# Turning a third diagonal of score blocks by DMA, with z brought in as fp32 and the query copies dropped

## The chip, the cores and the metric

The kernel runs on one core of one Trainium2 chip. The metric is the device time of one execution in microseconds (us). The core's engines are TensorE (PE; its weight loads are shown as PEld), VectorE (DVE), ScalarE (ACT), GpSimd (POOL) and SyncE (SP), which does nothing here but issue DMAs. All DMAs of the core, whichever engine issues them, are carried out by 16 DMA engines.

## The reference

Two layers follow one another, over 8 batches of 3200 tokens, with a width of 256 and a head size of 64:

```python
scores = (1.0 / S) * np.matmul(z, z.transpose(0, 2, 1))        # z: 8 x 3200 x 64
x = u * np.matmul(np.maximum(scores, 0.0) ** 2, v)             # u, v: 8 x 3200 x 256
wq, wk = x @ w_q, x @ w_k                                      # 256 -> 64
mixed = np.einsum('bst,btd->bsd', (1/8) * np.einsum('bsd,btd->bst', wq, wk), x)
out = np.maximum(mixed, 0.0) @ w_out                           # 8 x 3200 x 256, float32
```

The scores of a batch are symmetric, since both factors are z. The second layer has no nonlinearity between its two products, so the kernel sums the keys times x first (a 64 x 256 matrix per batch, called the heads here) and multiplies the queries with that.

## The kernel before

**Tiles.** A batch's 3200 tokens make seven groups of columns, six of 512 and one of 128 (`widths`, numbered 0 to 6; the last is `LASTG`), and 25 rows of 128. A score tile is one row of 128 by one group of columns. For a group, the kernel needs all 25 rows: they are the weights of the second product, in 128x128 pieces, with the matching row of v as the moving operand (L289, 100 matmuls of 256 columns for a group of 512).

**Scored or turned.** Because the scores are symmetric, a block that was scored for group gi and belongs to the rows of group gj serves group gj too, transposed. `is_turned` says for which pairs of groups that is done: up to two groups further on (`FAR`), and for the last group always. Such a block goes through a DMA transpose (L268) from the tile `at` into a tile `tt` (tags tt1 and tt2 by distance, with 3 and 4 buffers; ttl for the last group), and the later group reads its weights from there. All other tiles are scored by PE (L211). The contraction of a score matmul is 64 long, so z is held twice, on both halves of the partitions (`zT`), and the two matmuls of a pair run on the two halves of the array.

**Stages of a pair.** Two score tiles share one PSUM tile (three of them, `pps`). The first stage (DVE L234 or ACT L230) takes the positive part into the fp32 tile `g`; the second stage (POOL L249 or ACT L247), one pass later, squares it into the fp16 tile `at` (14 buffers); then the transposes of its turned blocks are issued on SP.

**The loop.** Nothing is scheduled by the compiler; the program's order is what each engine executes. The main loop makes one pass after another, number k. A pass scores six tiles (four where it also mixes), runs the first stage of these pairs and the second stage of those of the pass before, and lets PE do a share of the second product of the group in hand, on tiles scored two passes before (`LAG`). After ten of its matmuls one further piece of work can stand: a round of keys, or the mixing of one group of the batch before. `at_phase` holds what is due at the start of a pass: loads of u, and loads, doubling and turning of z, and loads of v for the next batch.

**Gate and keys.** When a group is complete, `gate` multiplies the two accumulators with u on DVE (L315), and x is turned by DMA (`xT`, L327). Five passes later or more, `keys_and_heads` projects x to queries and keys (L337), ACT copies them (L348), SP turns the keys (`kx`, L353). In the pass of the next round, `double_keys_queries` copies the queries to the other half of the partitions by a DMA on SP (L361) and the keys within `kx` on POOL (L362); PE then multiplies these keys and x (`heads`, L368), and DVE adds the sums over the groups (L379, L381; after the last group L387 makes `hs`).

**Mixing.** Once a batch's heads are complete, its groups are mixed one by one in the passes of the next batch: two matmuls (L416), one for each half of the width, on the two halves of the array, a ReLU on ACT (L428), the output projection (L441), a scaling (L468 or L463) and the store on SP (L469). The last group of 128 goes beside the key rounds (`side_mix`, `side_proj`).

**z.** The first batch's z is loaded as fp32 in four pieces and turned by PE. Later ones come by one casting DMA on POOL's queue into half of `zd` (L131), DVE doubles it (L134), and SP turns all of it with one DMA transpose (L138). `zd` has one buffer.

**Behind the loop** the last batch's heads come from a Gram matrix of x (`last_gram`, `last_heads`), and the rest of the mixing of the last two batches follows.

## Time and profile before

| | |
|---|---|
| Median of 3 runs | 807.75 us (806.59 to 809.63) |
| The profiled execution | 807.18 us, its span 805.4 us |
| Granted TensorE clock | 0.999 |
| Busy share of PE, DVE, ACT, POOL | 98%, 61%, 59%, 60% |
| Score matmuls (L211) | 920 |
| Second product (L289) | 5000 matmuls of 273 ns: weights from `at` 3656, from `tt` 1152, from `ttl` 192 |
| DMA | 330,878 packets, 143.20 MB; under 512 bytes 307,441 |

The spans are measured from the first to the last instruction. Matmuls overlap in their pipeline, so the mean of one (273 ns) is longer than its distance to the next. "Idle before" is the time in which an engine did nothing ahead of an instruction, with what ended it. The share of the DMA engines adds up the durations of their packets over 16 engines; packets of two queues can overlap, so it can pass 1.

### The profile page before, as it was taken

The page shows a single profiled execution, that of the slowest core. Times are in us where ns is not written, and L with a number is a line of the kernel's source. Part 1 is how long each engine was busy: PE and PEld are TensorE (multiplying, and loading weights), DVE is VectorE, ACT ScalarE, POOL GpSimd, SP SyncE. Part 2 cuts the span into 40 slices and gives each one's busy share as a digit, 9 for nine tenths or more (in the row PEclk, how much of TensorE's full clock was granted, in tenths as well). Part 3 has the DMA queues.
Part 4 walks back from the last instruction along what each step waited for, and adds up shares of the span by engine and source line. Part 5 has one row for each costly group of instructions (what it writes and reads, how often), then busy time and mean ns, then how long its engine had stood idle before and what let it go on. Part 6 is the DMA issues. An engine that isn't in the chain of part 4 may idle for free.

```text
span 805.4 us, 16696 instructions
## 1 busy us (share of the span) xinstructions
PE 788.8 (98%) x6778; PEld 584.9 (73%) x6778; DVE 493.1 (61%) x514; ACT 475.1 (59%) x526; POOL 485.2 (60%) x352
## 2 busy tenths in 40 slices
PE   7999999999999999999999999999999999999996
PEld 4777777777777777777777777777777767767774
DVE  5766666565665566755676556765666656655525
ACT  6655556556765556565675556656665565565534
POOL 7957676564666557755666466864676555655420
PEclk9999999999999999999999999999999999999999
DMA  7999899997989969998899979999999996867436
GB/s 175 149 198 192 141 176 181 212 190 134 216 148 208 200 152 194 176 208 186 175 157 211 198 157 178 188 206 175 184 197 157 182 217 143 159 148 183 116 98 246
DMA packets 330878, 143.20 MB, mean 178 GB/s; under 512 B 307441, under 2 KB 313137, under 8 KB 330801
## 3 DMA queue, kind: packets, MB, share of 16 engines
q1 hardware_dynamic: 302528, 125.90, 76.4%
q0 software_dynamic: 28128, 15.98, 17.7%
q8 instruction: 53, 0.87, 0.5%
q10 hardware_dynamic: 144, 0.26, 0.1%
q14 instruction: 25, 0.20, 0.1%
HBM read 59.38 MB, written 26.21 MB: 106 GB/s over the span
## 4 chain that ended last, share of the span: by engine, by line
PE 95%; issue 1%; POOL 1%; DMA 1%; DVE 1%; ACT 0%; SPq 0%; POOLq 0%; DVEq 0%
PE acc L289 69%; PE sc L211 13%; PE fo L441 5%; PE qk L368 3%; PE qk L337 3%; PE mx L416 2%; POOL at L249 1%; DMA z<-in_z_dram 1%; DMA xT_sb<-x_sb 0%; DVE x_sb L315 0%; DVE fo L463 0%; PE qk L499 0%; ACT qk L348 0%; SPq L95 0%; DVE g L234 0%
## 5 line engine op out<-in xcount | busy, mean ns | idle before, releaser
L249 POOL TENSOR_TENSOR at<-g 128x1024 f16<-128x1024 f32 (+2 forms) x234 | 430.3, 1853 | 222.2 <-DVE g L234 136.8
L234 DVE TENSOR_SCALAR g<-sc 128x1024 f32<-128x1024 f32 (+1 forms) x340 | 388.1, 1184 | 188.5 <-PE sc L211 188.1
L289 PE MATMUL acc<-v_sb,at 128*128 128x256 f16 x3656 | 446.8, 273 | 0.4 <-DVE x_sb L315 0.4
L289 PEld LDWEIGHTS <-at 128*128 128x128 f16 x3656 | 344.7, 98 | 108.0 <-issue 66.6
L230 ACT ACTIVATE g<-sc 128x1024 f32<-128x1024 f32 x128 | 131.2, 1025 | 199.6 <-PE sc L211 199.6
L247 ACT ACTIVATE at<-g 128x1024 f16<-128x1024 f32 (+2 forms) x234 | 236.9, 1029 | 0.6 <-DVE g L234 0.6
L289 PE MATMUL acc<-v_sb,tt 128*128 128x256 f16 x1152 | 149.1, 273 | 0.0
L211 PE MATMUL sc<-zT 64*128 64x512 f16 x920 | 129.7, 381 | 2.3 <-DVE hs L387 0.9
L289 PEld LDWEIGHTS <-tt 128*128 128x128 f16 x1152 | 112.5, 98 | 12.9
L315 DVE TENSOR_TENSOR x_sb<-acc,u_sb 128x512 f16<-128x512 f32 (+1 forms) x104 | 69.3, 668 | 66.8 <-PE acc L289 62.5
L428 ACT ACTIVATE rt<-mx 128x1024 f16<-128x1024 f32 (+1 forms) x49 | 49.1, 1012 | 56.8 <-PE mx L416 55.3
L211 PEld LDWEIGHTS <-zT 64*128 64x128 f16 x920 | 34.9, 95 | 50.1 <-issue 28.5
L362 POOL COPY kx<-kx 128x256 f16<-128x256 f16 (+1 forms) x54 | 20.1, 378 | 65.9 <-DMA kx<-qk 65.7
L468 ACT ACTIVATE fo<-fo 128x1024 f32<-128x1024 f32 (+1 forms) x40 | 40.6, 1014 | 24.4 <-PE fo L441 22.6
L441 PE MATMUL fo<-wo,rt 128*128 128x256 f16 x386 | 49.6, 273 | 1.7 <-DVE fo L463 0.9
L348 ACT CAST qk<-qk 128x512 f16<-128x512 f32 (+1 forms) x54 | 28.7, 545 | 27.5 <-PE qk L368 13.2
L441 PEld LDWEIGHTS <-rt 128*128 128x128 f16 x386 | 37.2, 98 | 7.5 <-ACT rt L428 1.9
L381 DVE TENSOR_TENSOR ha<-ha,qk 128x256 f32<-128x256 f32 x31 | 13.1, 421 | 30.0 <-ACT qk L348 30.0
L368 PE MATMUL qk<-x_sb,kx 128*128 128x256 f16 x191 | 28.4, 273 | 1.9 <-POOL kx L362 1.9
L337 PE MATMUL qk<-xT_sb,wqk 128*128 128x512 f16 (+1 forms) x108 | 29.9, 358 | 0.0
L368 PEld LDWEIGHTS <-kx 128*128 128x128 f16 x195 | 19.0, 98 | 14.2 <-POOL kx L362 2.4
L289 PE MATMUL acc<-v_sb,ttl 128*128 128x256 f16 x192 | 22.6, 273 | 0.0
(47 smaller groups left out, 150.2 us busy)
## 6 DMA issues: line engine op xcount, KB each, us to landing
u_sb<-in_u_dram SPq DMA_DIRECT2D x48, 512.0 KB, 4.8
out_dram<-fo SPq DMA_DIRECT2D x46, 512.0 KB, 4.2
v_sb<-in_v_dram POOLq DMA_DIRECT2D x35, 320.0 KB, 5.7
qk<-qk SPq DMA_DIRECT2D x47, 64.0 KB, 4.0
zd<-in_z_dram POOLq DMA_DIRECT2D x7, 400.0 KB, 8.1
tt<-at SPq DMA_TRANSPOSE x146, 4.3
u_sb<-in_u_dram SPq DMA_DIRECT2D x8, 128.0 KB, 3.0
xT_sb<-x_sb SPq DMA_TRANSPOSE x56, 4.1
```

What stands on the lines that cost most here:

```text
L211: nc.tensor.matmul(out=sc[:, h, 0:gw], lhsT=zT[b][half : half + dqk, ts(ti, P)], rhs=zT[b][half : half + dqk, ds(gs, gw)], start=True, sto ...
L230: nc.scalar.activation(out=g[:, hs, 0:w], in_=sc[:, hs, 0:w], func=RELU, scale=GSCALE)
L234: nc.vector.tensor_scalar(out=g[:, hs, 0:w], in0=sc[:, hs, 0:w], scalar1=0.0, scalar2=GSCALE, op0=AOP.max, op1=AOP.mult,)
L247: nc.scalar.square(out=out, in_=g[:, hs, 0:w])
L249: nc.gpsimd.tensor_mul(out=out, in0=g[:, hs, 0:w], in1=g[:, hs, 0:w])
L289: nc.tensor.matmul(out=accs[j // 2][:, ds((j % 2) * D, D)], lhsT=weights(b, gi, ti, j), rhs=vs[b][:, ti, :], start=(first and ti == rows_[ ...
L315: nc.vector.tensor_mul(out=xs[b, gi][:, 2 * half : 2 * half + n, :].rearrange("p n d -> p (n d)"), in0=accs[half][:, 0 : n * D], in1=us[b, ...
L337: nc.tensor.matmul(out=out, lhsT=w[:, ac, :, :].rearrange("p t h -> p (t h)"), rhs=xTs[b, gi][:, 0 : gw // P, ac, :], start=(start and ac ...
L368: nc.tensor.matmul(out=ps[:, 1, 0:D], lhsT=ks[b, gi][:, n, :, :].rearrange("p a h -> p (a h)"), rhs=xs[b, gi][:, n, :], start=((gi, n) == ...
L428: nc.scalar.activation(out=rts[b, gi][:, :, 0:gw], in_=ps[:, :, 0:gw], func=RELU)
L441: nc.tensor.matmul(out=banks[jf // 2][:, ds((j - jf) * D, D)], lhsT=rt[:, dc, ts(j, P)], rhs=wo[:, dc, :], start=(dc == 0 and j == jf), st ...
L468: nc.scalar.mul(out=flat_out[:, sl], in_=part, mul=FINAL_SCALE)
```

## The change

- Blocks three groups further on are turned too, except in the last batch. All three distances now have `tt` tiles of three buffers. In a group's order of tiles, the blocks for the next group stand first, then those that only this group uses and those for groups further on; the last row fills the pair up.
- z of batches 1 to 7 comes as fp32 on SP's queue, in four pieces of six or seven rows; DVE casts each piece twice, into the two halves of a smaller `zd` of one buffer, after the first stages of a pass (`late`); SP turns each piece a pass later. The first batch's z is doubled in tiles of `at`'s pool.
- In odd groups and the last one the projection's weights are swapped (`wkq`), so the queries land on the other half of the partitions. The copies of queries and keys (`double_keys_queries`) are gone; the heads of even and odd groups are summed on different halves and added crosswise at the end of the batch (`heads_crossed`), with `hz`, half of it zero, for the last group.
- Mixing takes two groups side by side, one half of the width at a time; the two matmuls use the two halves of the array for the two groups. A mixing pass projects one finished group of `todo_proj`.
- The loads of v stand two passes earlier. The pools of `g` and `rt` have fewer buffers, the raw weights lie in a tile of x's pool, and the part behind the loop follows the new mixing.

The core of the diff:

```diff
@@ pools and the first batch's z @@
-    FAR = 2
-    pg = ctx.enter_context(tc.tile_pool(name="pg", bufs=8))
+    pg = ctx.enter_context(tc.tile_pool(name="pg", bufs=7))
-    prt = ctx.enter_context(tc.tile_pool(name="prt", bufs=3))
+    prt = ctx.enter_context(tc.tile_pool(name="prt", bufs=2))
+    ZP = [(0, 6), (6, 6), (12, 6), (18, 7)]
-    zd0 = pz.tile([P, NT, 2, dqk], FP16, tag="zd", name="zd")
...
+        zds[c] = pat.tile([P, nn, 2, dqk], FP16, tag="at", name="zd")
...
@@ z of the later batches @@
-    def load_z(b):
-        zds[b] = pz.tile([P, NT, 2, dqk], FP16, tag="zd", name="zd")
-        nc.gpsimd.dma_start(out=zds[b][:, :, 0, :], in_=rows(z, b))
-
-    def double_z(b):
-        nc.vector.tensor_copy(out=zds[b][:, :, 1, :], in_=zds[b][:, :, 0, :])
-
-    def turn_z(b):
-        zT[b] = pzt.tile([P, S], FP16, tag="zT2", name="zT2")
+    def load_z(b, i):
+        n0, nn = ZP[i]
+        z32[b, i] = pz.tile([P, 7, dqk], FP32, tag="z32", name="z32", bufs=2)
+        nc.sync.dma_start(out=z32[b, i][:, 0:nn, :], in_=rows(z, b)[:, n0 : n0 + nn, :])
+
+    def double_z(b, i):
+        nn = ZP[i][1]
+        zds[b] = pz.tile([P, 7, 2, dqk], FP16, tag="zd", name="zd")
+        for half in range(2):
+            nc.vector.tensor_copy(out=zds[b][:, 0:nn, half, :], in_=z32[b, i][:, 0:nn, :])
+
+    def turn_z(b, i):
+        n0, nn = ZP[i]
+        if i == 0:
+            zT[b] = pzt.tile([P, S], FP16, tag="zT2", name="zT2")
         nc.sync.dma_start_transpose(
-            out=zT[b][:].rearrange("p (n s) -> p n s", s=P),
-            in_=zds.pop(b)[:].rearrange("p n a k -> p (n a k)"),
+            out=zT[b][:, ds(n0 * P, nn * P)].rearrange("p (n s) -> p n s", s=P),
+            in_=zds[b][:, 0:nn, :, :].rearrange("p n a k -> p (n a k)"),
         )
...
@@ which blocks are turned, and the order of a group's tiles @@
-    def is_turned(gi, gj):
-        return gi < gj and (gj <= gi + FAR or gj == LASTG)
+    def is_turned(b, gi, gj):
+        far = 3 if b + 1 < B else 2
+        return gi < gj and (gj <= gi + far or gj == LASTG)
...
-            elif len(tiles) % 2:
-                order = own[:1] + near + own[1:]
             else:
-                order = near + own
+
+                single = [NT - 1]
+                order = [t for t in near if group_of(t) == gi + 1 < LASTG]
+                order += [t for t in own + near if t not in order + single]
+                order = single + order if len(tiles) % 2 else order + single
...
-                kind, nr, bufs = ("l", 1, 8) if gj == LASTG else (gj - gi, 4, gj - gi + 2)
+                kind, nr, bufs = ("l", 1, 8) if gj == LASTG else (gj - gi, 4, 3)
...
@@ keys, queries, heads @@
-        ks[b, gi] = pk.tile([P, 4, 2, dh], FP16, tag="kx", name="kx")
+        ks[b, gi] = pk.tile([P, 4, P], FP16, tag="kx", name="kx")
...
-    def double_keys_queries(b, gi):
-        gw = widths[gi]
-        nn = gw // P
-        nc.sync.dma_start(out=qks[b, gi][dh:P, 0:gw], in_=qks[b, gi][0:dh, 0:gw])
-        nc.gpsimd.tensor_copy(out=ks[b, gi][:, 0:nn, 0, :], in_=ks[b, gi][:, 0:nn, 1, :])
+    def swapped(gi):
+        return gi % 2 == 1 or gi == LASTG
...
     def heads_out(b, gis, ps):
+        mine = slice(0, dh) if swapped(gis[0]) else slice(dh, P)
...
+        acc, part = hacc[b][mine, :], ps[mine, 1, 0:D]
+        if gis[0] < 2:
+            nc.vector.tensor_copy(out=acc, in_=part)
         else:
-            heads_done(b, ps[:, 1, 0:D])
...
+            nc.vector.tensor_add(out=acc, in0=acc, in1=part)
+
+    def heads_crossed(b):
+
+        hx = psml.tile([P, D], FP32, tag="hx", name="hx", bufs=1)
+        nc.vector.tensor_copy(out=hx[0:dh, :], in_=hacc[b][dh:P, :])
+        nc.vector.tensor_copy(out=hx[dh:P, :], in_=hacc[b][0:dh, :])
+        return hx
+
+    def heads_done(b):
+        hx = heads_crossed(b)
         hss[b] = psml.tile([P, D], FP16, tag="hs", name="hs")
-        nc.vector.tensor_add(out=hss[b][:], in0=hacc.pop(b)[:], in1=part)
+        nc.vector.tensor_add(out=hss[b][:], in0=hacc.pop(b)[:], in1=hx[:])
+        nc.vector.tensor_copy(out=hz[b % 2][dh:P, :], in_=hss[b][dh:P, :])
...
@@ mixing @@
-    def mix(b, gi):
-        gw = widths[gi]
+    def mix(b, pair, db):
+
+        ps = ps_tile("mx")
+        for a in range(2):
+            half = a * dh
+            nc.tensor.matmul(
+                out=ps[:, a, :],
+                lhsT=hss[b][half : half + dh, ds(db * P, P)],
+                rhs=qks[b, 2 * pair + a][half : half + dh, :],
+                start=True,
+                stop=True,
+            )
+        return ps
...
@@ group_begun: what a batch's first pass makes due @@
-            due(k + later + 3, lambda: load_z(b + 1))
-            due(k + later + 9, lambda: double_z(b + 1))
-            due(k + later + 10, lambda: turn_z(b + 1))
+            for i, at in enumerate((1, 3, 6, 8)):
+                at += k + later // 4
+                due(at, lambda i=i: load_z(b + 1, i))
+                due(at + 3, lambda i=i: double_z(b + 1, i), late)
+                due(at + 4, lambda i=i: turn_z(b + 1, i))
             for i in range(5):
-                due(k + later + 5 + 3 * i, lambda i=i: load_v(b + 1, 5 * i, 5))
+                due(k + later + 3 + 3 * i, lambda i=i: load_v(b + 1, 5 * i, 5))
...
@@ the loop @@
-        if keying and keyed:
-            for g_ in keyed[0][1]:
-                double_keys_queries(keyed[0][0], g_)
         if mixing:
             mix_out(*mixing)
+            if mixing[2] == 1:
+                todo_proj.extend((mixing[0], 2 * mixing[1] + a) for a in range(2))
         staged = []
         act_pair = 0 if (gate_pending or k < 4) else 1
         for i, (p0, sc) in enumerate(fresh):
             on_act = i == act_pair and not mixing
             staged.append((p0, first_stage(p0, sc, on_act)))
+        for fn in late.pop(k, []):
+            fn()
...
-        if mixing:
-            mb, mg, _ = mixing
+        if mixing and todo_proj:
+            mb, mg = todo_proj.pop(0)
...
@@ behind the loop @@
+    for _ in range(min(2, len(todo_mix))):
+        mix_next()
+    psh = ps_tile("hd")
+    last_heads(last, g32, psh)
+    hss[last] = psml.tile([P, D], FP16, tag="hs", name="hs")
+    nc.vector.tensor_add(out=hss[last][:], in0=hx[:], in1=psh[:, 1, 0:D])
+    while todo_mix:
+        mix_next()
...
+    for pair in range(LASTG // 2):
+        for db in range(ND):
+            mix_out(last, pair, db, mix(last, pair, db), on_dve=(pair == 0 and db == 1))
+            if pair:
+                store(last, 2 * pair - 2 + db)
```

## The prediction

> **What bounds the kernel now.** First the page's engine line and the chain that ended last: is one engine busy throughout, and doing what?
>
> ```profile
> PE 788.8 (98%) x6778; PEld 584.9 (73%) x6778; DVE 493.1 (61%) x514; ACT 475.1 (59%) x526; POOL 485.2 (60%) x352
> PE 95%; issue 1%; POOL 1%; DMA 1%; DVE 1%; ACT 0%; SPq 0%; POOLq 0%; DVEq 0%
> PE acc L289 69%; PE sc L211 13%; PE fo L441 5%; PE qk L368 3%; PE qk L337 3%; PE mx L416 2%; POOL at L249 1%; DMA z<-in_z_dram 1%; DMA xT_sb<-x_sb 0%; DVE x_sb L315 0%; DVE fo L463 0%; PE qk L499 0%; ACT qk L348 0%; SPq L95 0%; DVE g L234 0%
> ```
>
> TensorE is the bound; DVE, ACT and POOL have 40% to spare. So a score matmul saved is time saved, if what replaces it (a DMA transpose) arrives in time. Next, therefore, the DMA side: the slices, the queues, one stage of the windows, and the issues.
>
> ```profile
> DMA  7999899997989969998899979999999996867436
> q1 hardware_dynamic: 302528, 125.90, 76.4%
> q0 software_dynamic: 28128, 15.98, 17.7%
> 220.00:320.00 100.00, 100.00 (x867) 74.31 (x865) 61.53 (x65) 60.44 (x67) 62.02 (x44) 1.00 1.01 181
> tt<-at SPq DMA_TRANSPOSE x146, 4.3
> zT<-zd SPq DMA_TRANSPOSE x7, 6.8
> qk<-qk SPq DMA_DIRECT2D x47, 64.0 KB, 4.0
> zd<-in_z_dram POOLq DMA_DIRECT2D x7, 400.0 KB, 8.1
> ```
>
> Behind a PE that never waits, the 16 DMA engines are full as well (share 1.01 in a steady stage). Last, SP's queue in the order of time, in the third batch (start, us, instruction), and one round of keys from the timeline of all engines:
>
> ```profile
> 221.40 2.49 SPq L353 DMA_TRANSPOSE kx<-qk  x2
> 223.94 0.57 SPq L146 DMA_DIRECT2D u_sb<-in_u_dram  x1
> 224.61 9.53 SPq L268 DMA_TRANSPOSE tt<-at  x4
> 234.23 1.23 SPq L268 DMA_TRANSPOSE ttl<-at  x1
> ...
> 246.09 3.99 SPq L138 DMA_TRANSPOSE zT<-zd  x1
> ...
> 255.48 0.59 PE L337 MATMUL qk<-xT_sb,wqk 128*128 128x512 f16 x2
> ...
> 265.69 1.22 SPq L353 DMA_TRANSPOSE kx<-qk  x1
> ...
> 268.19 0.40 POOL L362 COPY kx<-kx 128x256 f16<-128x256 f16 x1 [5.31 <-DMA kx<-qk]
> ...
> 271.26 0.60 PE L368 MATMUL qk<-x_sb,kx 128*128 128x256 f16 x4
> ```
>
> SP issues without a pause here. The turn of zT belongs to the pass of the main loop whose first score starts at 239.3; SP gets to it at 246.09, 6.8 us late, and three passes on it is 9.8 us late (a copy due at 253.6 is issued at 263.44). The keys projected at 255.5 reach SP at 265.7, land near 268.2, and are multiplied at 271.3: 3 us to spare. PE is not waiting, but SP's queue is close to being what it waits for.
>
> **The gain.** Tiles scored per batch by group are now 25, 21, 17, 17, 17, 17, 1 = 115. Turning also three groups further takes four each from groups 3, 4 and 5: 103. It holds for batches 0 to 6: 7 × 12 = 84 of 920 score matmuls go. Six of them take 0.75 us from their start to the next product (268.98 to 269.73 in PE's timeline), so 84 × 0.125 = 10.5 us; at the chain's 13.5% of 805.4 / 920 = 118 ns it would be 9.9. The second product keeps its count, only its operand comes from `tt` instead of `at` (both rows 273 ns). Mixing has as many matmuls as before. DVE, ACT and POOL lose 42 pairs, off the path.
>
> **Edits on other engines.** POOL loses 54 copies of kx (20 us) and seven z issues (1.6 us each). DVE gets 56 small casts of z (an fp32 128x256 cast took 294 ns; near 0.4 us each, 22 us) for seven copies of 1.34 us, which hide in its 39% idle time unless they wait (below). Crossing the two halves of the heads adds two copies and an add ahead of the first mix, at 0.42 us each 1.26 us; in the trace hs ends 1.26 us ahead of that matmul in five of seven batches, so 0 to 0.3 us each: nothing taken, 2 us in the range. The tail has one more group of the batch before to project and store (0.87 us on PE, which leaves the loop); its pairs need both ReLUs before the first store: +0.5 us net, 0 to 2. The smaller pools (7 `g`, two pairs of `rt`) only matter when a reader is late; taken at nothing.
>
> **The DMA balance.** By the trace's packet records a 256-byte packet takes 24.8 ns on average. A 128x1024 transpose is 1024 of them over 16 engines: 1.58 us; the 42 new ones are 66 us of all 16 engines. z leaves POOL's queue (22,400 packets of 128 bytes, 35.5 ns: 50 us) and comes as fp32 on SP's (3,584 packets at the 90 ns of the first batch's z: 20 us); the 54 copies of q (61 ns a packet) take 11.5 with them. Net +25 us over seven batches, but SP's own queue, served in order, gets +75.
>
> The Trainium skill, "DMA: Bandwidth & Descriptors", section Specifications, gives about 27 GiB/s per engine and warns that transfers under 512 bytes stay below line rate. At its full rate the new transposes would cost an estimated 24 us, not 66. The rows side with the warning: 256 bytes in 24.8 ns are 10 GB/s, 4096-byte loads run at 20 (200 ns).
>
> **Where it bunches.** The new blocks are made by groups 0 to 2 of each batch, in which group 0 and 1 passes are the shortest on PE. I count the fourth batch from the second pass of group 0 to the second of group 2, nine passes. PE: 240 second-product matmuls at 112.5 ns (32 take 3.60 in the chain) 27.0, scores 9 × 0.75 = 6.8, two mixes and three key rounds 4.5: 38.3 us. SP's queue: 18 tt 28.4, two ttl and four kx at 0.79 4.7, two xT 3.2, two of z's turns 2.5, four z loads 2.8, three u 4.8, two stores 3.2: 49.6, and three v loads beside them on POOL's queue, 7.1: 56.7 us of packets. How fast does that go? From 209.8 to 246.1 packets worth 40.4 us went out in 36.3, a ratio of 0.90; from 240.15 to 278.6, 40.7 in 38.5, 0.95. So 51 us, 13 more than PE has, where the same group of passes before ended 7 us late. Lower bound: if only issue counts (tt 1.29, kx 1.22, loads 0.4 to 0.6 us), 43 us, 5 more.
>
> **What waits for that.** Two things. First the keys: the kx of the sixth of these passes has 35.8 us of packets ahead of it, 32.2 us at 0.90, against 20.4 us of PE; with 1 us of lateness at the start it is issued 12.8 us after its pass begins, lands (median 3.4) at 16 to 17, and the heads want it at 15: PE waits about 2 us, more directly than before, as POOL's copy no longer stands between. Second a new wait: z's pieces share one `zd` buffer, so DVE's cast of a piece waits until the turn of the piece before has landed, and on DVE the gates, the head sums and the next pass's first stages queue behind it. The last cast stands one pass after the third turn. Late by 12 us (13 and 1, less the 2 already waited) and landing 3.5 after issue, that turn is done 15.5 us after its pass starts; DVE comes to the cast at 8.7 (5.7 of the pass, 3.0 to the end of the first stages in the next): 6.8 us late. Of that some 2.5 are DVE's idle gap in a pass (2.0 to 2.7 in the timeline); about 4 reach PE through the score buffers. By 0.90 a batch loses 6 us; by 0.95 8; by issue alone 0, the lateness then fitting the gap. I take 5, nearer the rows of a full queue. In groups 3 to 5 SP has 28 us of work in 36 and recovers.
>
> **Sum.** The profiled execution was 807.18 (span 805.4). 807.18 − 10.5 + 7 × 5 + 0.5 = 832.2. The median of the runs is 0.57 above the profiled one: 832.8, say 833. 0.5%, 4 us, is about what a measurement of this kernel can tell from no change.
>
> **Rivals.**
> *The queue copes.* The stall is nil, as with issue alone; for it: PE waits for no DMA today with SP up to 10 us late, new blocks are needed groups later, and copies of q and the slow 128-byte packets are gone. Against: the counted bunch and the single `zd`. It decides while SP is under 7.7 us late at the third turn (8.7 + 2.5 − 3.5). 807.75 − 10.5 + 0.5 = 797.8, down to 796 with nothing lost in the tail. Chance 0.26. By the skill's 27 GiB/s this is how it would come out; 10 GB/s in the rows bears that out little.
> *It cancels.* 1 to 2 us a batch: 804 to 812. Chance 0.06.
> *DMA sets the pace altogether.* At 0.95 and with `at` buffers held by late transposes (POOL and ACT then wait too), 8 us a batch: 854, with the heads' 2 us 856. Chance 0.18 inside the slower case; it decides where a transpose lands over about 19 us after its second stage, when the fourteenth next pair, 4.7 passes of 4.1 us on, needs the buffer.
> *It doesn't do what it says:* the `tt` two groups on have three buffers, not four; if the fourth block waits for the first's reading, SP's whole queue stands behind it. By the order of tiles the reading is a pass earlier, so this adds to the slower case and has no number of its own.
>
> **How the numbers follow.** Slower 0.68 (0.50 the forecast, 815 to 848; 0.18 the last), same 0.06, faster 0.26. Range 796 to 857: the low end takes in the coping queue, the high end the DMA-bound case.
>
> **What would show it.** Right: L211 x836; its saved time matched by new PE idle time in groups 1 to 3 of each batch, ended by DMA kx or by DVE's g; DVE waiting at the cast of zd on a DMA zT, some 7 us at the last piece; SP late by over 10 us there. Wrong: PE at 98% or more and a span near 796, or DVE's cast never waiting. If PE waits for hs or in the tail instead, the mechanism is another.

## The result, and the profile after

The changed kernel takes 880.73 us (median of six runs, 871.94 to 886.13), the kernel before 809.31 in the same comparison: a ratio of 1.0855, interval 1.0808 to 1.0902. The forecast was 833, its range ended at 857. The direction was right, the size was not: a loss of 71 us where 25 were expected. The profiled execution took 872.33 us, near the lower end of the six; its span is 870.5. Here and in the tables below, a run more than 1.5% above its kernel's fastest counts in the median and not in the ratio.

The page of the changed kernel, the same parts as before (engines; granted clock and DMA by slices; the two queues; the chain that ended last):

```profile
PE 795.3 (91%) x6694; PEld 590.3 (68%) x6694; DVE 497.4 (57%) x566; ACT 438.1 (50%) x493; POOL 420.2 (48%) x273
...
PEclk9998999999999999999999999998999989999999
DMA  8999778985999759998599996999769996688536
...
q1 hardware_dynamic: 347264, 139.45, 76.9%
q0 software_dynamic: 5616, 13.11, 11.0%
...
PE 65%; DVE 6%; DMA 6%; issue 4%; ACT 2%; SPq 1%; DVEq 0%; ACTq 0%
PE acc L305 47%; PE sc L227 8%; PE fo L496 4%; DMA zT<-zd 4%; DVE g L250 2%; PE qk L390 2%; PE qk L356 2%; PE mx L448 1%; DMA kx<-qk 1%; DVE zd L138 1%; DVE x_sb L331 1%; SPq L284 1%; DVE fo L518 1%; ACT at L263 1%; DMA kx<-ql 0%
```

PE is no longer busy throughout, and the chain now runs through the turn of z (4%) and the transposed keys. The 16 DMA engines are not fuller than before: the slices dip to 5 and 6 once a batch. Something waits in a circle, and then nobody has work.

The groups (in each line, behind the second bar, the idle time of the engine before the group and what ended most of it):

```profile
L227 PE MATMUL sc<-zT 64*128 64x512 f16 (+1 forms) x836 | 120.7, 384 | 20.4 <-DVE g L250 9.9
L138 DVE CAST zd<-z 128x384 f16<-128x384 f32 (+1 forms) x56 | 33.8, 645 | 93.3 <-DMA zT<-zd 70.8
L390 PE MATMUL qk<-x_sb,kx 128*128 128x256 f16 x191 | 30.5, 286 | 13.6 <-DMA kx<-qk 12.2
L356 PE MATMUL qk<-xT_sb,wkq 128*128 128x512 f16 x46 | 15.3, 419 | 20.0 <-DVE g L250 20.0
```

The 84 score matmuls are gone (836). DVE stands idle for 93.3 us ahead of the casts of z: 13 us a batch. PE, in turn, waits for DVE's first stages (scores and projections take their PSUM tiles from the same pool, and a tile is free again when its first stage is done) and for the keys. The waits (in total, times, longest, all in us but the count):

```profile
DVE zd L138 <- DMA zT<-zd: 70.8, 13, 11.1
...
DVE zd L138 <- issue: 22.5, 5, 10.2
...
PE qk L356 <- DVE g L250: 20.0, 3, 7.2
PEld L390 <- DMA kx<-qk: 14.5, 5, 5.5
...
PE qk L390 <- DMA kx<-qk: 12.2, 4, 5.0
PE sc L227 <- DVE g L250: 9.9, 5, 5.9
```

SP's queue in the fourth batch, where it issues from 327 to 404 us with no pause of more than some tenths (start, us, instruction):

```profile
347.62 1.88 SPq L144 DMA_TRANSPOSE zT<-zd  x1
349.56 0.63 SPq L152 DMA_DIRECT2D u_sb<-in_u_dram  x1
350.28 7.15 SPq L284 DMA_TRANSPOSE tt<-at  x3
...
366.46 1.24 SPq L144 DMA_TRANSPOSE zT<-zd  x1
...
376.38 7.27 SPq L284 DMA_TRANSPOSE tt<-at  x3
383.75 2.12 SPq L375 DMA_TRANSPOSE kx<-qk  x1
385.96 1.24 SPq L144 DMA_TRANSPOSE zT<-zd  x1
...
395.14 1.25 SPq L144 DMA_TRANSPOSE zT<-zd  x1
```

And one of its gaps, from the timeline of all engines:

```profile
384.62 0.60 PE L305 MATMUL acc<-v_sb,tt 128*128 128x256 f16 x4
...
385.96 1.24 SPq L144 DMA_TRANSPOSE zT<-zd  x1
...
388.82 1.15 DVE L138 CAST zd<-z 128x448 f16<-128x448 f32 x2 [8.64 <-DMA zT<-zd]
...
389.88 2.35 DVE L250 TENSOR_SCALAR g<-sc 128x1024 f32<-128x1024 f32 x2
...
391.14 1.01 PE L356 MATMUL qk<-xT_sb,wkq 128*128 128x512 f16 x2 [5.93 <-DVE g L250]
```

This is the circle. The third turn is issued at 385.96 and lands 2.8 us later; DVE had been waiting 8.64 us for it, with the first stages of the pass queued behind the cast; PE waits 5.9 us for those. The first three turns are issued 19 us apart, though the pieces are planned two or three passes (8 to 14 us) apart. The first turn took 7.3 us to land, at 354.9, and the second cast starts at 355.0; the second landed at 369.2, and the third cast starts at 369.3. So in this batch every piece but the first waits for the turn ahead of it, and each of the next two turns stands behind eight or nine other transposes in SP's queue. Over all seven batches the last piece always waits, 7.2 to 11.1 us and 65 of the 93 us together; the two pieces ahead of it wait in eleven of fourteen cases, 28 us together. The waits that the list puts down to "issue" end with the landing of a turn too.

One more loss is in the clock: 0.974 of the full clock in the profiled execution, where before it was 0.999. Around the gap just shown (a stretch, its length, busy us of PE, PEld, DVE, ACT and POOL with counts, then granted clock, DMA share, GB/s):

```profile
384.00:391.00 7.00, 1.22 (x12) 0.94 (x11) 2.18 (x3) 1.88 (x2) 0.00 (x0) 0.84 0.96 182
391.00:394.00 3.00, 2.85 (x13) 1.81 (x13) 1.34 (x3) 0.59 (x1) 2.77 (x2) 0.50 1.05 203
394.00:397.00 3.00, 3.00 (x22) 2.38 (x21) 1.00 (x2) 1.33 (x2) 0.97 (x1) 0.73 0.59 117
```

PE idles for 6 us and then works at half the clock for some microseconds. The trace has eight such spells ahead of the end, some 41 us together; before had none there. So the engine lines give the whole account. PE's work at nearly the full clock is 779.4 us (its busy time in e15 below, with as many matmuls at a clock of 0.995; e7 has 779.8), 9.4 less than the 788.8 of before: the gain, forecast as 10.5. The changed kernel has 795.3: 15.9 more, most of it by the slow clock: in all its slow spells, with the one at the very end, PE is busy for 27 us, and half of that is 13.5. Its idle time is 870.5 − 795.3 = 75.2 us against 16.6: 58.6 more. −9.4 + 15.9 + 58.6 = 65.1, the difference of the two spans.

### The profile page after: what moved, and what is told of

The parts are those of the page before. It is cut to its first block, busy times and chain, and to the rows that moved or that the text cites. A ratio compares the mean times of both kernels' runs of the same rounds, so it can differ in the third digit from the quotient of the medians.

```text
span 870.5 us, 16494 instructions
## 1 busy us (share of the span) xinstructions
PE 795.3 (91%) x6694; PEld 590.3 (68%) x6694; DVE 497.4 (57%) x566; ACT 438.1 (50%) x493; POOL 420.2 (48%) x273
## 4 chain that ended last, share of the span: by engine, by line
PE 65%; DVE 6%; DMA 6%; issue 4%; ACT 2%; SPq 1%; DVEq 0%; ACTq 0%
PE acc L305 47%; PE sc L227 8%; PE fo L496 4%; DMA zT<-zd 4%; DVE g L250 2%; PE qk L390 2%; PE qk L356 2%; PE mx L448 1%; DMA kx<-qk 1%; DVE zd L138 1%; DVE x_sb L331 1%; SPq L284 1%; DVE fo L518 1%; ACT at L263 1%; DMA kx<-ql 0%
## 5 line engine op out<-in xcount | busy, mean ns | idle before, releaser
L265 POOL TENSOR_TENSOR at<-g 128x1024 f16<-128x1024 f32 (+1 forms) x212 | 392.4, 1862 | 411.2 <-DVE g L250 253.2
L250 DVE TENSOR_SCALAR g<-sc 128x1024 f32<-128x1024 f32 (+2 forms) x309 | 356.2, 1195 | 136.8 <-PE sc L227 135.6
L305 PE MATMUL acc<-v_sb,at 128*128 128x256 f16 x3320 | 412.1, 275 | 6.9 <-DVE x_sb L331 6.8
L305 PEld LDWEIGHTS <-at 128*128 128x128 f16 x3320 | 315.2, 98 | 107.2 <-issue 70.1
L246 ACT ACTIVATE g<-sc 128x1024 f32<-128x1024 f32 (+2 forms) x117 | 116.2, 995 | 237.1 <-PE sc L227 235.1
L305 PE MATMUL acc<-v_sb,tt 128*128 128x256 f16 x1488 | 189.8, 276 | 0.0
L305 PEld LDWEIGHTS <-tt 128*128 128x128 f16 x1488 | 147.8, 99 | 18.7
L227 PE MATMUL sc<-zT 64*128 64x512 f16 (+1 forms) x836 | 120.7, 384 | 20.4 <-DVE g L250 9.9
L138 DVE CAST zd<-z 128x384 f16<-128x384 f32 (+1 forms) x56 | 33.8, 645 | 93.3 <-DMA zT<-zd 70.8
L469 ACT ACTIVATE rt<-mx 128x1024 f16<-128x1024 f32 x47 | 48.0, 1023 | 65.2 <-PE mx L448 64.8
L390 PE MATMUL qk<-x_sb,kx 128*128 128x256 f16 x191 | 30.5, 286 | 13.6 <-DMA kx<-qk 12.2
```

The source lines that it names most:

```text
L138: nc.vector.tensor_copy(out=zds[b][:, 0:nn, half, :], in_=z32[b, i][:, 0:nn, :])
L227: nc.tensor.matmul(out=sc[:, h, 0:gw], lhsT=zT[b][half : half + dqk, ts(ti, P)], rhs=zT[b][half : half + dqk, ds(gs, gw)], start=True, sto ...
L246: nc.scalar.activation(out=g[:, hs, 0:w], in_=sc[:, hs, 0:w], func=RELU, scale=GSCALE)
L250: nc.vector.tensor_scalar(out=g[:, hs, 0:w], in0=sc[:, hs, 0:w], scalar1=0.0, scalar2=GSCALE, op0=AOP.max, op1=AOP.mult,)
L265: nc.gpsimd.tensor_mul(out=out, in0=g[:, hs, 0:w], in1=g[:, hs, 0:w])
L305: nc.tensor.matmul(out=accs[j // 2][:, ds((j % 2) * D, D)], lhsT=weights(b, gi, ti, j), rhs=vs[b][:, ti, :], start=(first and ti == rows_[ ...
```

## The experiments

Each is timed against the kernel before on the same chip; the ratio has its 95% interval in brackets. "Before" and "after" name the kernel that was edited.

**1. Four kernels: the single buffer, the third diagonal, z's way, and the third diagonal alone.**

e1: after, z's doubled pieces in `at`'s pool (14 buffers) in place of the single `zd`.

```diff
-        zds[b] = pz.tile([P, 7, 2, dqk], FP16, tag="zd", name="zd")
+        zds[b] = pat.tile([P, 7, 2, dqk], FP16, tag="at", name="zd")
```

> The changed kernel, but each piece of z is cast into a tile of the pool of `at` (14 buffers) in place of the single `zd`. Theory A (the single buffer is the cost): DVE's 93 us of waits at the cast vanish, the clock returns to 0.99 or more, and the time is 797 to 805 us. Theory B (SP's queue and the DMA engines have more work from group 0 to 2 than PE): the waits at the cast vanish too, but PE then waits for keys (kx), for late blocks or for `at` buffers, SP's queue still runs without a pause for some 70 us of each batch, and the time is 830 to 870.

e2: after, without the third diagonal.

```diff
-        far = 3 if b + 1 < B else 2
+        far = 2
```

> The changed kernel with blocks up to two groups further turned, as before (42 transposes fewer, 84 score matmuls more); z, q, mixing and pools stay changed. Theory A: the cast still waits for each turn of z, so most of the loss stays: over 840 us. Theory B: with the transposes gone SP keeps up, each turn lands before the next cast, and the time is 805 to 815.

e3: after, z as before: one casting load by POOL, one doubling copy on DVE, one turn.

```diff
-            for i, at in enumerate((1, 3, 6, 8)):
...
+            due(k + later + 3, lambda: load_z(b + 1))
+            due(k + later + 8, lambda: double_z(b + 1), late)
+            due(k + later + 9, lambda: turn_z(b + 1))
```

> The changed kernel with z of later batches as before: one casting DMA on POOL's queue, one doubling on DVE, one turn on SP; the third diagonal stays. No piece waits for another. Theory A: 797 to 805 us. Theory B: SP has four loads less but the 128-byte packets are back on the same DMA engines: 830 to 870 us, with PE waiting for keys.

e4: before, with the third diagonal and nothing else of the change but the three buffers for each `tt` tag (the tag two groups on had four).

```diff
-    def is_turned(gi, gj):
-        return gi < gj and (gj <= gi + FAR or gj == LASTG)
+    def is_turned(b, gi, gj):
+        far = 3 if b + 1 < B else 2
+        return gi < gj and (gj <= gi + far or gj == LASTG)
```

> The kernel before with the third diagonal alone (batches 0 to 6; three buffers for each distance), its order of tiles and all else as before. Theory A: 797 to 802 us, as nothing waits for zd. Theory B: SP's queue, with the copies of q still in it, falls further behind than in the changed kernel: 840 us or more, POOL's copies of kx and PE waiting for DMA.

| | us | ratio |
|---|---|---|
| e1 | 850.09 | 1.0533 [1.0481, 1.0585] |
| e2 | 842.81 | 1.0437 [1.0394, 1.0480] |
| e3 | 865.90 | 1.0624 [1.0557, 1.0692] |
| e4 | 835.67 | 1.0346 [1.0291, 1.0401] |

e1: the casts no longer wait for a turn, and the kernel gains some 30 us. So taking the single buffer away is worth 30 us, and e1 is still 41 over the kernel before. What waits now (e1, the waits):

```profile
PEld L390 <- DMA kx<-qk: 29.8, 11, 4.8
...
PE qk L390 <- DMA kx<-qk: 24.4, 11, 4.3
```

The keys, eleven times instead of four: with one circle opened, SP's queue and the DMA engines are what is late.

e4 tells why. It has no new wait at DVE, and still the third diagonal alone costs 27 us. Its DMA engines by slices, its stage from 420 us on, and its waits:

```profile
DMA  8999799999999989999999999999999999877536
```

```profile
420.00:520.00 100.00, 97.81 (x836) 73.49 (x835) 56.27 (x59) 54.91 (x62) 53.78 (x40) 0.98 1.14 197
```

```profile
POOL kx L363 <- DMA kx<-qk: 180.2, 35, 12.4
...
PE qk L369 <- POOL kx L363: 19.4, 7, 6.5
PE sc L212 <- DMA zT<-zd: 7.0, 1, 7.0
```

The slices have no gap left between the batches; the share is 1.14 in this stretch, the highest of seven such stretches (0.98 to 1.14, where before had 0.88 to 1.08); both queues of e4 together hold 82.4 + 18.0 = 100.4% of the 16 engines over the whole span (before 94.1%). In us that is 832 against 758: 74 more, and the prediction had 66 for the new transposes. Before had 47 us left in its span. The prediction's rival of the `tt` buffers has hardly a sign here: of SP's waits ahead of the blocks' transposes one, of 3.1 us, ends with PE's reading.

e3 shows that z's new way is not the root: with z back on POOL's queue and only one turn a batch, PE waits 45.1 us for keys. (Its profiled execution took 870.06 us, of runs from 853.80 to 870.70, so these waits are read for their kind.)

e2 came out where theory A had it, over 840: without the third diagonal the kernel is still 34 us slower than before. DVE's waits at the cast are down from 93.3 to 27.9 us, in nine waits, and each of them ends some 0.1 us after the landing of a turn, those too that the list puts down to "issue". The same line shows a second suspect, the casts themselves:

```profile
L138 DVE CAST zd<-z 128x384 f16<-128x384 f32 (+1 forms) x56 | 44.8, 841 | 27.9 <-issue 20.7
```

0.84 us each where 0.4 were forecast, 45 us of DVE in the middle of its passes.

**2. The casts off DVE, and packets taken away.**

e5: e2, with z as in e3.

> The changed kernel without the third diagonal and with z as before (POOL's casting DMA): what is left are the swapped queries and keys, the crossed heads, mixing by pairs, the smaller pools, v two passes earlier. Theory B (the transposes and z's pieces cost, the rest doesn't): 803 to 812 us. Theory C (the crossed heads and the pairs cost as well, since e2 was still 35 us above the kernel before): 820 us or more.

e6: e2, with e1's buffers and the casts on ACT.

```diff
-            nc.vector.tensor_copy(out=zds[b][:, 0:nn, half, :], in_=z32[b, i][:, 0:nn, :])
+            nc.scalar.copy(out=zds[b][:, 0:nn, half, :], in_=z32[b, i][:, 0:nn, :])
```

> As e2 (two groups further, z in four pieces on SP's queue), but each piece is cast by ACT in place of DVE, into tiles of the pool of `at`. If e2's loss is DVE's (casts of up to 2 us and waits for the turn ahead of gates and first stages): 803 to 815 us. If it is the four loads and turns in SP's queue: 825 to 845.

e7: e1, with v loaded for the first batch alone.

```diff
+        vs[b] = vs[0]
+        return
```

> As e1, but v is loaded for the first batch alone and used for all (POOL's 35 loads of v are left out, so the sums of later batches are not the reference's). If the 16 DMA engines are the limit in groups 0 to 2: packets fall by 7 us in 57 per window, SP's issues return to 1.29 us, waits for kx shrink to a third or less, 805 to 820 us. If SP's issuing alone is the limit: the time stays within 1.5% of e1's 850.

e8: e1, with the casts on ACT and the pieces of z later in the batch.

```diff
-            for i, at in enumerate((1, 3, 6, 8)):
+            for i, at in enumerate((5, 6, 9, 10)):
```

> The third diagonal with z's pieces in tiles of `at`'s pool, cast by ACT, and loaded, cast and turned four to five passes later (loads due at 5, 6, 9, 10), towards groups 3 to 5 where SP has room. By theory B the window of groups 0 to 2 loses some 5 us of z's DMAs: 815 to 835 us, waits for kx about half of e1's. If the time stays at 845 or more, z's place in the queue does not matter.

| | us | ratio |
|---|---|---|
| e5 | 825.26 | 1.0180 [1.0126, 1.0234] |
| e6 | 819.58 | 1.0144 [1.0115, 1.0172] |
| e7 | 810.93 | 1.0036 [1.0019, 1.0053] |
| e8 | 859.85 | 1.0634 [1.0608, 1.0660] |

e5 is at 820 or more, as theory C had it: what is left of the change costs something too. e6, between its two forecasts, is 23 us faster than e2 with the same DMAs in the same places: that much of e2's loss was DVE casting, and waiting to cast. As e6 takes the single buffer away with the casts, it does not part the two. On ACT a cast takes 0.52 us with little spread, and no wait of PE in the loop passes 2.5 us:

```profile
L138 ACT CAST zd<-z 128x384 f16<-128x384 f32 (+1 forms) x56 | 26.4, 521 | 0.5 <-DMA z<-in_z_dram 0.5
```

e7 is the clearest. SP issues the same 522 DMAs as in e1, the matmuls are the same, DVE casts as slowly (843 ns); only 35 loads are missing, and those are on POOL's queue. 39 us come back. The same hundred microseconds as above, in e1 and then in e7:

```profile
420.00:520.00 100.00, 96.94 (x830) 72.86 (x829) 61.20 (x69) 53.44 (x60) 49.74 (x32) 0.98 1.02 200
```

```profile
420.00:520.00 100.00, 99.89 (x869) 75.55 (x867) 66.01 (x72) 56.88 (x64) 50.32 (x29) 1.00 0.94 189
```

The time that SP spends issuing falls from 667 to 622 us, with the same instructions: a transpose took 1.69 us to issue in e1 on average, 1.54 in e7 (the median is near 1.28 in both). So SP is slowed by packets of another queue, and not by the number of its own instructions.

That does not make the 16 engines full throughout. The two queues of e1, and then those of e17 (section 5, a kernel with one new block and z as before):

```profile
q1 hardware_dynamic: 347264, 139.45, 82.3%
q0 software_dynamic: 5616, 13.11, 10.9%
```

```profile
q1 hardware_dynamic: 317312, 129.57, 80.1%
q0 software_dynamic: 28128, 15.98, 18.2%
```

e1's make 93.2% of its span of 845.9, or 788 us, which would fit into the 805.4 of before; e17's make 98.3% of 808.7, or 795 us, and e17 loses nothing. So the sum over the span accounts for e4, and not for e1. Why e1 loses 41 us at a load that e17 carries, no run here separates: the place of the new blocks, z's way and the rest of the change all differ. (e7 also leaves out the issuing of the 35 loads on POOL, 0.6 us each, 21 us of an engine that idles half the time.)

e8 came out above its first forecast: placed later, the pieces come too late, and PE waits for them (15.6 us, four times) beside the keys (20.1 us). Nothing was won.

**3. The parts one by one, and the mended kernel.**

e9: before, with z as fp32 on SP in four pieces, cast by ACT into tiles of `at`'s pool.

> The kernel before with one part of the change: z of later batches as fp32 by SP's queue in four pieces, but cast by ACT into tiles of `at`'s pool. It takes 50 us of 128-byte packets off the DMA engines and adds 20 us on SP's queue. If the DMA engines' load is what matters: no stall, 802 to 809 us, DMA share of a steady stage 0.95 or less. If SP's queue order matters more: keys land later than before, 812 to 825.

e10: e9, with two of the three new blocks (1 to 4, 2 to 5).

```diff
+        third = b + 1 < B and gj == gi + 3 and gi != 0
+        return gi < gj and (gj <= gi + FAR or gj == LASTG or third)
```

> As e9, and two of the three blocks a third group on are turned too (groups 1 to 4 and 2 to 5; 28 transposes or 44 us of DMA more, 56 score matmuls or 7 us of PE less). Load on the engines 14 us over the kernel before: if a full DMA side is the limit, 805 to 820 us, the gain of 7 eaten; if the freed packets carry it, 797 to 803, faster than both.

e11: e1, with the casts on ACT and v's loads later.

```diff
-                due(k + later + 3 + 3 * i, lambda i=i: load_v(b + 1, 5 * i, 5))
+                due(k + later // 2 + 5 + 3 * i, lambda i=i: load_v(b + 1, 5 * i, 5))
```

> The whole change mended where the runs showed waits: z's pieces in tiles of `at`'s pool and cast by ACT (as e8, but loaded at the change's own passes 1, 3, 6, 8), and v loaded about two passes later, as before. The third diagonal stays. If the DMA engines are the limit in groups 0 to 2: 825 to 845 us, waits for kx still over 15 us, as only their order changes. If the waits were DVE's: 800 to 812.

e12: e5, with v's loads where they were before.

```diff
-                due(k + later + 3 + 3 * i, lambda i=i: load_v(b + 1, 5 * i, 5))
+                due(k + later + 5 + 3 * i, lambda i=i: load_v(b + 1, 5 * i, 5))
```

> As e5 (swapped queries, crossed heads and pairs alone), with v loaded at the passes of before. If e5's waits for kx come from v's loads standing earlier: 810 to 818 us, kx waits under 3 us. If not: within 0.5% of e5's 825.

| | us | ratio |
|---|---|---|
| e9 | 812.22 | 1.0103 [1.0061, 1.0146] |
| e10 | 835.41 | 1.0353 [1.0332, 1.0373] |
| e11 | 848.55 | 1.0523 [1.0499, 1.0548] |
| e12 | 814.99 | 1.0102 [1.0080, 1.0123] |

Before was 806.38 in this comparison. z's new way alone costs 5.8 us even with the casts off DVE (e9), just inside what its expectation had if SP's queue order matters more than the load: its two queues hold 746 us of packets, before 758. e12, which keeps of the change the queries' halves, the crossed heads, the pairs of groups, the order of the tiles and the smaller pools, with z's copy and turn planned one pass earlier, costs 8.6. What PE waits for most there, after the start of the program:

```profile
PE mx L442 <- DVE hs L412: 3.9, 3, 1.4
```

That is the crossing ahead of the first mix: up to 1.4 us each time, 3.9 of the 8.6, where the prediction took nothing and kept 2 us in its range; the rest is not traced to one part. Against e5 it also says that v two passes earlier costs 6 us by the ratios, 10 by the medians.

Four terms then add up: the third diagonal 27.1 (e4), z 5.8 (e9), the rest 8.6 (e12), the single buffer 880.73 − 850.09 = 30.6; together 72.1, measured 71.4. Two kernels test the sum in part: without the third diagonal and the single buffer it gives 820.8, and e6 has 819.6; with all but the single buffer 847.9, and e11 has 848.6. It is a ledger of costs found by separate edits, and that it closes so well is partly chance. The terms are not independent: z's new way costs 5.8 us without the third diagonal, and with it e14 (below) is 22 us faster than e13, which has z as before. The ledger also has no entry for v two passes earlier (6 us against e5) and none for the casts on DVE, which cannot be told from the single buffer in e2, and of which nothing can be seen between e1 and e11, which moves v as well.

e10 and e11 missed both their forecasts, upwards. e10: two thirds of the blocks, with z's new way, cost as much as e4 with all of them, although its profiled execution has the two queues at 91.7% of the span. e11: with the waits at the casts taken away and v later, PE waits for keys 34.0 us. Mending these waits did not bring the time back.

**4. Is it the keys, or the packets?** The keys are the one DMA that PE wants within two passes of its issue. If only they were late, it would do to want them later.

e13: e4, with the heads using the keys of two rounds back, and buffers to match.

```diff
-    px = ctx.enter_context(tc.tile_pool(name="px", bufs=5))
-    pk = ctx.enter_context(tc.tile_pool(name="pk", bufs=3))
+    px = ctx.enter_context(tc.tile_pool(name="px", bufs=6))
+    pk = ctx.enter_context(tc.tile_pool(name="pk", bufs=4))
...
-        if keyed:
+        if len(keyed) > 1:
```

> As e4 (the kernel before with the third diagonal alone), but the heads take the keys of two rounds ago, not of one (six passes or more after the projection in place of three; one more buffer each for x, kx and the queries, one fewer for g). If PE's waits for kx (19 us of e4's 32 us of gaps, with the clock they lower) are where the third diagonal's gain goes: 797 to 812 us. If the DMA side is simply too slow, the wait moves to zT, x's turn or the blocks, and the time stays at 825 or more.

e14: e13, with z as in e9.

> As e13, with z in four pieces on SP's queue, cast by ACT into tiles of `at`'s pool (as e9): some 30 us of packets less. If packets decide: 3 to 10 us faster than e13. If SP's order decides: as e13 or slower.

e15: e4, with v loaded for the first batch alone, as in e7.

> As e4, with v loaded for the first batch alone and used for all batches (35 loads of v left out; the sums of later batches are not the reference's). It asks whether the 10.5 us of score matmuls are saved at all once the DMA side has room: 796 to 800 us if so; 815 or more if something else than the DMA engines holds e4.

e16: before, with the keys of two rounds back as in e13, and no further block turned.

> The kernel before with the keys two rounds back alone, as a control for e13: within 0.5% of the kernel before, since its waits for kx are 2 us in all; more if the longer hold of x and of the queries makes ACT or the gate wait.

| | us | ratio |
|---|---|---|
| e13 | 842.92 | 1.0381 [1.0296, 1.0466] |
| e14 | 820.38 | 1.0119 [1.0047, 1.0190] |
| e15 | 803.04 | 0.9945 [0.9928, 0.9962] |
| e16 | 805.46 | 0.9977 [0.9965, 0.9989] |

The keys alone fell: e13 is no faster than e4. The lateness moves on to what is wanted next, z (16.8 us in two waits) and the last group's queries (11.8). e14 takes packets away (z's 22,400 small ones for 3,584 larger) and gains 22 us, more than the 3 to 10 that were expected if packets decide; e15 takes v's away and is 0.5% faster than before, a little short of the 796 to 800 us expected. Its engine line, and all that PE waits for beyond 4 us:

```profile
PE 779.4 (97%) x6694; PEld 584.2 (73%) x6694; DVE 459.2 (57%) x483; ACT 440.1 (55%) x495; POOL 429.3 (54%) x295
```

```profile
PE sc L214 <- DMA zT<-zd: 6.0, 1, 6.0
```

So the third diagonal does save its matmuls, 9.4 us of PE, and without v's loads of seven batches nothing eats the saving whole. No run leaves v's loads out of the kernel before, so how much of e15's gain is theirs is not shown. e16 is a complete kernel, 0.2% below before, as its expectation had it: taking the keys later costs nothing, and hardly gains.

**5. One block in place of three.** Two kernels on e16, with one new block each: e17 turns 0 to 3 in batches 0 to 6, e18 turns 2 to 5.

```diff
+        third = b + 1 < B and gj == gi + 3 and gi == 0
+        return gi < gj and (gj <= gi + FAR or gj == LASTG or third)
```

> As e16, and of the third diagonal only the block of groups 0 and 3, in batches 0 to 6: 14 transposes (22 us of packets) more and 28 score matmuls (3.5 us) less. Its transposes fall at the start of a batch, where SP's queue has room. If the place in the batch decides: 800 to 804 us, 3 us under e16. If any further transpose costs more than it saves: over 806.

> As e17, but with the block of groups 2 and 5, whose transposes fall into the passes in which SP is latest. By the bunching: slower than e17 by 3 to 10 us. If only the number of packets counts: the same as e17 within 2 us.

| | us | ratio |
|---|---|---|
| e17 | 805.70 | 0.9975 [0.9954, 0.9996] |
| e18 | 812.55 | 1.0039 [1.0009, 1.0068] |

Neither earns its matmuls (28 × 0.125 = 3.5 us) beyond what e16 had. e17 stands between its two forecasts, e18 where the bunching had it. The same number of transposes costs 5 us more by the ratios, 7 by the medians, in one place of the batch than in the other, with a large scatter (e17 801.70 to 810.83, e18 804.09 to 822.23). Which wait makes the difference stays open: e18's profiled execution was its fastest, 804.09 us, and shows PE waiting for no DMA longer than 1.7 us.

## Why the prediction was wrong in size

**The gain** held: forecast 10.5, 9.4 measured in PE's busy time (e15), 836 score matmuls.

**The kind of loss** held. Named were the keys late behind a bunch of transposes, and DVE's cast behind the turn ahead of it with the first stages queued behind; both are in the profile after, and both rivals without a stall fell: the queue that copes, since e4 has only the third diagonal and loses 27 us, and the cancelling case. The third rival, DMA setting the pace altogether, at 854 to 856, came nearest in number, and the measured 881 lies beyond it. Its mechanism is not what the changed kernel shows: its two queues hold 87.9% of the span, and POOL waited 4.0 us in all for a buffer of `at` that a transpose of blocks held, ACT not at all. Of the signs that the prediction asked for, DVE's wait at the last piece was to be some 7 us and is 9.3 on average over the seven batches (8.6 in the fourth).

**The step that failed is the term 7 × 5 = 35 us for the stall.** In the profiled execution it measured 58.6 us of idle time and 15.9 of longer work of PE: 74.5, or 10.6 a batch, with all that had been taken at nothing inside. The term was made of two waits, about 4 us a batch at the cast and 2 at the keys, and taken a little below their sum. Set against the runs:

1. *The late transfers apart from the cast were mis-sized most.* They were priced by the keys alone, 14 us in all. e1, with no wait at the cast left, is still 41 us over before. e4, the third diagonal without any of the change's casts, loses 27.1 us after saving the 9.4 of the matmuls: 36.5 us. In its trace PE waits at the keys (19.4 us) and at z (7.0), and the clock falls to 0.983. Why lateness costs that much more than the 14 is not traced further.
2. *The single buffer was counted at one cast of four.* I took only the last cast as late, by 6.8 us, and set 2.5 against it for DVE's idle time. DVE waited 13 us a batch: 9.3 at the last cast and 4 at the two before it. I worked out one late turn from the queue as the plan fills it. But the cast's lateness delays the first stages, these the transposes, and the next turn stands behind those: the circle can carry the lateness into the next piece. By e1 the buffer is worth 30.6 us, near the 28 of seven times 4. That is partly luck: the waits were longer than forecast, and taking them away lets the wait for the keys grow from 12.2 to 24.4.
3. *The casts were priced by one row from a quiet place.* 0.4 us, from a cast of the first batch's z at 0.294; they took 0.645 on average, up to 2.046. They were to hide in DVE's idle time; but a cast stands ahead of the first stages of the next pass, and those PE waits for. Casts and single buffer together cost 23 us without the third diagonal (e2 to e6); the casts' own share stays open.
4. *The clock was left out.* Every gap of PE was taken at its own length; most of the 15.9 us is the slow clock behind the gaps.
5. *Terms "taken at nothing".* The crossing, the pairs, the pools: 8.6 us (e12). z's way was counted as a relief: alone it loses 5.8 us (e9), with the third diagonal it relieves (e13 to e14, 22 us).

**The DMA balance** was right in size: 66 us for the transposes (e4 has 74 more in its queues), and +25 for the whole change, where the changed kernel's two queues hold 765 us and e1's 788, against 758 before. For the third diagonal alone the sum over the span, 94.1% taken with 47 us left for 74 more, is in the page's queue lines and tells the loss without any stage; e4's slices show no recovery in groups 3 to 5. For the whole change that sum would have fitted, as the prediction has it, and the slices do dip once a batch: what failed there is what the lateness costs, not the balance. The Trainium skill, "DMA: Bandwidth & Descriptors", section Latency and other measured facts, gives DMA transposes 261 to some 400 GB/s; the prediction's rows have 1.58 us of 16 engines for 256 KB, 166 GB/s, and e4's growth is of that size. By the Trainium skill's rate the new transposes would take an estimated 28 to 42 us and would have fitted.

**The keys** were forecast at 2 us a batch, 14 together, and PE waited 12.2 at them. The agreement is luck in part: it is four waits of up to 5.0 us, not one in each batch, in a kernel whose PE the casts hold back; in e1 it is 24.4. And the tail, taken at 0.5, made no difference that a run here separates.

## What to carry to other kernels

Before moving work from a busy engine to DMA, add up the queues' shares over the whole span. Where the new transfers do not fit into what is left, as in e4, the loss is plain from that sum. Where they fit, as in the changed kernel, it proves nothing yet: look at the stretch in which they bunch, and price every wait behind it, not the first one alone. A load on POOL's queue can slow the transposes on SP's (e1 to e7). A cast that waits for a DMA is badly placed in the in-order queue of an engine that feeds the DMAs ahead of it; give the pieces buffers enough that nobody waits. Removing the wait that a profile names moved it to the next consumer here (e1, e13); what brought time back was taking packets away (e7, e14, e15), though not in e9.

## What the runs showed of the hardware

**DVE's casts end with POOL's squares.** The casts of the changed kernel take 0.347 us or up to 2.046. From the timeline of POOL, and of DVE, in the fourth batch:

```profile
342.12 3.86 POOL L265 TENSOR_TENSOR at<-g 128x1024 f16<-128x1024 f32 x2 [2.74 <-ACT g L246]
```

```profile
343.45 2.74 DVE L138 CAST zd<-z 128x384 f16<-128x384 f32 x2
```

The first cast starts while POOL's first square runs, the second while its second does. Of the 56 casts, 15 start beside a running square, and every one of them ends 213 to 217 ns after that square does; these take 1.20 us on average, the other 41 0.44. The Trainium skill, "SBUF — State Buffer", section Who interferes with whom, has the rule: a cast on DVE in a 2-port mode and an operation on GpSimd share a pair of ports, and whoever comes second is blocked until the first is done. The trace agrees, to 4 ns, though in which mode the casts ran it does not show; the prediction could have used it. ACT's casts in e6, beside the same squares, take 0.50 to 0.57 us.

**A gap of PE costs more than itself.** The eight spells of the changed kernel at a granted clock of 0.50 stand at gaps of PE of 2.2 to 7.2 us and last beyond them: four of 6.8 us at the four gaps of 5.9 to 7.2, four of 3.4 us at gaps of 2.2 to 5.0. Three gaps of 2.4 to 2.8 us have none. The runs' times follow the clock: of the changed kernel's, the one of 871.94 us had 0.976, the one of 881.29 had 0.965.

**The queues are not separate in cost.** Leaving out 35 loads on POOL's queue, of 320 KB each, took 45 us off SP's issuing and 39 off the kernel (e1 to e7).
